# Half of a group's first layer by seven half-size products instead of eight, from the third group of tokens on

## The chip, the cores and the metric

The kernel is one program on one core of a Trainium2 chip. The metric is the device time of one execution in microseconds (us); for a kernel the median of several executions is given. A core has five engines that run their own instruction streams in order and wait for each other through semaphores: PE (TensorE, matrix products, with PEld its weight loads), DVE (VectorE), ACT (ScalarE), POOL (GpSimd) and SP (SyncE, which here issues all transfers). SBUF is the on-chip memory that they share; PSUM is a small memory of eight banks (128 x 512 floats each) into which PE writes and from which ACT and DVE read.

## What is computed

The program does attention inside chunks of 64 positions, and then a two-layer network on each of the 4608 tokens:

```python
scores = scale * np.matmul(q_c, k_c.transpose(0, 1, 2, 4, 3))   # chunks of 64, 8 batches x 8 heads x 9 chunks
attn = softmax(scores); out = np.matmul(attn, v_c)
x = out.transpose(0, 2, 1, 3).reshape(4608, 512)
h = x @ w_in                 # 512 x 2048, the first layer
g = h - np.tanh(h)
return g @ w_out             # 2048 x 512, the second layer
```

All inputs and the output are 32-bit floats. The kernel reaches their precision with two halves for each operand: a number is written as high part plus low part, and a product is three matmuls (high x high, low x high, high x low).

## The kernel before

**Tiling.** The tokens are cut into 36 tiles of 128 (a tile is called a pair, since it holds two chunks), and these into 9 groups of 4 tiles, so a group is 512 tokens. The 2048 hidden units are cut into 16 slices of 128, called `fc`. One unit of work is one `fc` for one group.

**First layer** (`gemm1`, line 413): twelve matmuls in 16-bit floats, each 128 x 128 weights by 512 tokens: four slices of the 512 inputs, each with three combinations of high and low parts. They sum in one PSUM bank `ph`, of which there are two.

**Between the layers** (`shrink`): ACT takes the tanh from `ph` into `t` (line 421), DVE forms `ph - t` (422), ACT rounds the result to the high part `gh` (425), DVE takes the rest `gl` (426). **Second layer** (`gemm2`, line 434): for each of the group's four tiles three matmuls, 128 x 128 by 512 columns, in a 32-bit form (`fp32r`), into one of the four PSUM banks `po0` to `po3`, which collect all 16 `fc`. `finish` copies them out and SP stores them (lines 457 to 461).

**Order.** `FeedForward.run` goes over the 16 units of a group. At each step it emits the first layer of unit *s* and its `shrink`, then, since `LAG = 2`, the second layer of unit *s* - 2. The list `queue` holds the units whose second layer is still to come. Between these, `interleaved` sets pieces of the *next* group's attention (class `Late`) at fixed half steps (`BASE`, `LATER`, `STEPS`): `sums` of absolute values by ACT (96) whose maximum over all partitions POOL takes (103, `power`), `split` into high and low 16-bit parts (307 to 317), `scores` by PE (325), `softmax` on DVE and ACT (331 to 339), a rounding and a transpose by DMA (345 to 348), `values` by PE (359), and the copy of the result into the next group's operand `xh`, `xl` (362, 363).

**The first group** is different: the weights arrive as raw 64-bit words that DVE and ACT convert (`merged`, `weights`), while the attention of groups 0 and 1 runs (class `Early`). The list `PLAN` gives the order of that part; up to its bar PE and SP follow it literally. The scale of each pair of weight slices and of each group's values comes from `power`, that is from one POOL instruction (line 103), whose result DVE waits for (105).

**Who sets the order elsewhere.** Outside such literal stretches a scheduler orders each engine's stream by priority and by what it takes to be ready; the order is fixed when the program is built.

Of the kernel before, what the change touches and what calls it, by code (L numbers as in the profile page):

```python
# [11 lines left out]
F32 = mybir.dt.float32  # L12
# [3 lines left out]
U32 = mybir.dt.uint32  # L16
AF = mybir.ActivationFunctionType
ALU = mybir.AluOpType
# [19 lines left out]
RAW = 3  # L38
EARLY_FC = 8
# [6 lines left out]
BASE = (3, 9, 15, 21)  # L46
LATER = (8, 13, 18, 23)
STEPS = (0, 3, 4, 5, 10)
# [6 lines left out]
def attn_ffn_kernel(ctx: ExitStack, tc: tile.TileContext, qE, kE, vE, qL, kL, vL, w_in, w_out, out):  # L55
# [13 lines left out]
    ps_h = ctx.enter_context(tc.tile_pool(name="ps_h", bufs=2, space=PSUM))  # L69
    ps_a = ctx.enter_context(tc.tile_pool(name="ps_a", bufs=2, space=PSUM))  # L70
# [18 lines left out]
    def new_x():  # L89
        return tuple(xpool.tile([P, KC, MOST], F16, name=f"x{a}") for a in "hl")  # L90

    def spread(pool, a, out):

        shape = [a.shape[0], *a.shape[1:]]
        junk = pool.tile(shape, BF16, name=f"junk{math.prod(shape[1:])}", bufs=1)
        nc.scalar.activation(junk, a, AF.Abs, scale=2.0 ** -12, accum_out=out)  # L96
# [66 lines left out]
    class Early:  # L163
# [96 lines left out]
        def result(self, p, x, i):  # L260
            xh, xl = x
            d = self.st.pop(p)
            ps, to = d["vps"], d["to"]
            ts = slice(i * P, (i + 1) * P)
            nc.scalar.activation(xh[:, :, ts], ps, AF.Copy, scale=to)
            nc.vector.scalar_tensor_tensor(out=xl[:, :, ts], in0=ps, scalar=to, in1=xh[:, :, ts], op0=ALU.mult, op1=ALU.subtract)

    class Late:
# [4 lines left out]
        def __init__(self, pool):  # L273
            self.pool, self.st = pool, defaultdict(dict)
            self.raw = {n: pool.tile([P, MOST // P, H * CH], F32, name=f"raw{n}", bufs=1) for n in "qkv"}
            self.v16 = [[pool.tile([P, 2, 4, P], F16, name=f"v16{a}{i}", bufs=1) for a in "hl"] for i in range(2)]
            self.q16 = [[pool.tile([P, H, P], F16, name=f"q16{a}{i}", bufs=1) for a in "hl"] for i in range(2)]
            for t in self.v16[0] + self.v16[1] + self.q16[0] + self.q16[1]:
                nc.gpsimd.memset(t, 0.0)

        def load(self, p, i):
            for n, src in (("q", qL), ("k", kL), ("v", vL)):
                nc.sync.dma_start(out=self.raw[n][:, i], in_=src[p - NE])

        def sums(self, g, n):

            d = self.st[f"g{g}"]
            if n == "q":
                d["sums"] = self.pool.tile([P, 3], F32, name="sums", bufs=2)
            some = self.raw[n][:, :SIZES[g]]  # L290
            spread(self.pool, some, d["sums"][:, "qkv".index(n):"qkv".index(n) + 1])
            if n != "v":
                return
            d["to"], d["from"] = (self.pool.tile([P, 3], F32, name=m, bufs=2) for m in ("to", "from"))
            power(self.pool, "x", d["sums"], d["to"], d["from"])
            d["exp"] = self.pool.tile([P, 1], F32, name="exp", bufs=2)
            nc.vector.scalar_tensor_tensor(out=d["exp"], in0=d["from"][:, 0:1], scalar=scale, in1=d["from"][:, 1:2], op0=ALU.mult, op1=ALU.mult)  # L297
            from_x[g] = d["from"][:, 2:3]

        def split(self, g, p, i):  # L300
            d, to = self.st[p], self.st[f"g{g}"]["to"]
            d["exp"] = self.st[f"g{g}"]["exp"]
            q, k = (self.raw[n][:, i].rearrange("p (h c) -> p h c", h=H) for n in "qk")
            qh, ql = self.q16[p % 2]
            for c in range(2):
                r = slice(c * CH, (c + 1) * CH)
                nc.scalar.activation(qh[r, :, r], q[r], AF.Copy, scale=to[r, 0:1])  # L307
                nc.vector.scalar_tensor_tensor(out=ql[r, :, r], in0=q[r], scalar=to[r, 0:1], in1=qh[r, :, r], op0=ALU.mult, op1=ALU.subtract)  # L308
            kk = d["k"] = self.pool.tile([P, 2, H, CH], F16, name="k16", bufs=2)
            nc.scalar.activation(kk[:, 0], k, AF.Copy, scale=to[:, 1:2])  # L310
            nc.vector.scalar_tensor_tensor(out=kk[:, 1], in0=k, scalar=to[:, 1:2], in1=kk[:, 0], op0=ALU.mult, op1=ALU.subtract)
            v = self.raw["v"][:, i].rearrange("p (a d) -> p a d", d=D)
            vh, vl = (t.rearrange("p c hp d -> p (c hp) d") for t in self.v16[p % 2])
            for u in range(2):
                r = slice(u * D, (u + 1) * D)
                nc.scalar.activation(vh[r, :, r], v[r], AF.Copy, scale=to[r, 2:3])  # L316
                nc.vector.scalar_tensor_tensor(out=vl[r, :, r], in0=v[r], scalar=to[r, 2:3], in1=vh[r, :, r], op0=ALU.mult, op1=ALU.subtract)  # L317

        def scores(self, p):
            d = self.st[p]  # L320
            ps = d["ps"] = ps_a.tile([P, H, CH], F32, name="psa")
            q = self.q16[p % 2]
# [18 lines left out]
        def transpose(self, p):  # L341
# [5 lines left out]
            aT = self.pool.tile([P, 8, P], F16, name="aT", bufs=1)  # L347
# [3 lines left out]
        def values(self, p, x, i):  # L351
            d = self.st.pop(p)
            xh, xl = x
            ps = ps_a.tile([P, 4, 2, CH], F32, name="psa")
            for hp in range(4):
                for c in range(2):
                    cs = slice(c * CH, (c + 1) * CH)
                    for k, (a, b) in enumerate(((0, 0), (0, 1), (1, 0))):
                        nc.tensor.matmul(ps[:, hp, c, :], lhsT=self.v16[p % 2][a][:, c, hp, :], rhs=d["a16"][:, b, hp, cs], start=(k == 0), stop=(k == 2))  # L359
            ts = slice(i * P, (i + 1) * P)  # L360
            ps = ps.rearrange("p hp c k -> p hp (c k)")
            nc.scalar.mul(xh[:, :, ts], ps, 2.0 ** -14)
# [233 lines left out]
```

## Time and profile before

| | |
|---|---|
| median of 3 runs | 894.82 us (892.93 to 894.85) |
| profiled execution | 890.42 us, its span (first to last instruction) 888.3 us |
| PE busy | 866.5 us of the span (98%), 5163 matmuls |
| DVE busy | 538.5 us (61%) |
| ACT busy | 471.3 us (53%) |
| POOL busy | 15.5 us (2%) |
| mean granted clock of PE | 0.989 of full speed |

The profiled execution is one run, with the chip's profiler on; it lies 4.4 us under the median. A row such as `504.26 1.04 PE L413 MATMUL ph<-xh,wih 128*128 128x512 f16 x4` of the timeline says: from 504.26 us on, 1.04 us long, four matmuls of line 413, which write `ph` from `xh` and `wih`. What stands in brackets at a row's end is how long the engine sat idle just before, and whose signal ended that. Matmuls overlap (the next is fed while the last drains), so their pace is read from start to start, not from a row's length.

### The profile page before, as it was taken

How to read it: one execution, taken by the hardware profiler on the slowest of the kernel's cores; microseconds unless marked ns; L12 is line 12 of the kernel's file. 1: busy time of each engine (PE TensorE's matmuls, PEld its weight loads, DVE VectorE, ACT ScalarE, POOL GpSimd, SP SyncE). 2: the span in 40 equal slices, each digit the busy share in tenths (PEclk: the TensorE clock that was granted, in tenths of full speed). 3: DMA queues.
4: the chain of work that ended last, by engine and by line, in shares of the span. 5: the costliest groups of instructions: out<-in, count | busy, mean ns of one | idle time of the engine just before them, and what ended most of it. 6: DMA issues, size and time to landing. Idle time of an engine off the chain costs nothing.

```text
span 888.3 us, 13109 instructions
## 1 busy us (share of the span) xinstructions
PE 866.5 (98%) x5163; PEld 566.8 (64%) x5163; DVE 538.5 (61%) x976; ACT 471.3 (53%) x824; POOL 15.5 (2%) x32
## 2 busy tenths in 40 slices
PE   7999898999999999999999999999999999999997
PEld 4786655566656666666666666666666666665665
DVE  6798896667666665656466745674567456533222
ACT  8589773756646544555455634663366344423221
POOL 0000003000000000000000000000000000000000
PEclk8899999999999999999999999999999999999999
DMA  9584333312221121212112211132111100010001
GB/s 261 184 233 133 136 122 121 117 36 66 78 83 51 34 72 61 61 47 72 60 53 53 74 60 37 49 89 66 37 48 24 60 13 13 13 54 6 1 1 48
DMA packets 61373, 62.71 MB, mean 71 GB/s; under 512 B 32640, under 2 KB 40832, under 8 KB 61312
## 3 DMA queue, kind: packets, MB, share of 16 engines
q1 hardware_dynamic: 61312, 61.88, 23.8%
q8 instruction: 40, 0.66, 0.3%
q14 instruction: 21, 0.17, 0.1%
HBM read 45.09 MB, written 9.44 MB: 61 GB/s over the span
## 4 chain that ended last, share of the span: by engine, by line
PE 91%; ACT 4%; issue 2%; DVE 2%; DMA 0%; POOL 0%; ACTq 0%; DVEq 0%; POOLq 0%
PE po L434 42%; PE ph L413 40%; PE psa L359 2%; PE psa L325 2%; PE psa L258 2%; PE psa L210 1%; ACT junk L96 1%; ACT s L228 1%; PE ph L501 1%; ACT wih L152 0%; ACT w_out L126 0%; ACT s L241 0%; DVE w_out L127 0%; PE psa L160 0%; ACT w_in L126 0%
## 5 line engine op out<-in xcount | busy, mean ns | idle before, releaser
L434 PE MATMUL po<-woh,gh 128*128 128x512 f32 x576 | 245.6, 426 | 3.3 <-ACT gh L425 3.3
L434 PE MATMUL po<-wol,gh 128*128 128x512 f32 x576 | 225.9, 392 | 0.0
L434 PE MATMUL po<-woh,gl 128*128 128x512 f32 x576 | 225.8, 394 | 0.0
L422 DVE SCALAR_TENSOR_TENSOR t<-ph,sig,t 128x512 f32<-128x512 f32 (+1 forms) x148 | 108.7, 734 | 146.7 <-ACT t L421 146.5
L413 PEld LDWEIGHTS <-wih 128*128 128x128 f16 x1184 | 106.4, 98 | 137.4 <-issue 25.7
L421 ACT ACTIVATE t<-ph,sig 128x512 f32<-128x512 f32 (+1 forms) x148 | 99.8, 674 | 168.0 <-PE ph L413 167.7
L426 DVE TENSOR_TENSOR gl<-t,gh 128x512 fp32r<-128x512 f32 (+1 forms) x148 | 99.8, 675 | 111.4 <-ACT gh L425 111.2
L413 PE MATMUL ph<-xh,wih 128*128 128x512 f16 (+1 forms) x592 | 150.8, 377 | 5.5 <-ACT wih L152 5.5
L425 ACT CAST gh<-t 128x512 fp32r<-128x512 f32 (+1 forms) x148 | 89.4, 604 | 126.0 <-PE po L434 101.5
L413 PE MATMUL ph<-xh,wil 128*128 128x512 f16 (+1 forms) x592 | 149.3, 375 | 0.2 <-DVE wil L153 0.2
L413 PE MATMUL ph<-xl,wih 128*128 128x512 f16 (+1 forms) x592 | 148.5, 373 | 0.0
L434 PEld LDWEIGHTS po<-woh,gh 128*128 128x128 f32 x576 | 108.5, 188 | 34.4 <-ACT gh L425 5.7
L434 PEld LDWEIGHTS po<-woh,gl 128*128 128x128 f32 x576 | 108.0, 188 | 24.5 <-DVE gl L426 0.5
L434 PEld LDWEIGHTS po<-wol,gh 128*128 128x128 f32 x576 | 108.5, 188 | 21.5
L413 PEld LDWEIGHTS <-wil 128*128 128x128 f16 x592 | 58.0, 98 | 67.3 <-issue 1.1
L317 DVE SCALAR_TENSOR_TENSOR v16l<-rawv,to,v16h 64x512 f16<-64x512 f32 x56 | 41.8, 746 | 5.6 <-ACT v16h L316 4.7
L316 ACT ACTIVATE v16h<-rawv,to 64x512 f16<-64x512 f32 x56 | 40.1, 716 | 6.0 <-PE psa L359 4.5
L307 ACT ACTIVATE q16h<-rawq,to 64x512 f16<-64x512 f32 x56 | 40.3, 720 | 4.3 <-DVE exp L297 3.2
L308 DVE SCALAR_TENSOR_TENSOR q16l<-rawq,to,q16h 64x512 f16<-64x512 f32 x56 | 41.6, 744 | 1.3
L345 ACT CAST a<-s 128x512 f16<-128x512 f32 x28 | 17.3, 616 | 30.7 <-DVE s L339 27.9
L333 ACT ACTIVATE s<-s,exp 128x512 f32<-128x512 f32 x28 | 20.1, 719 | 17.2 <-DVE s L332 17.1
L457 DVE COPY t<-po 128x512 f32<-128x512 f32 x18 | 12.4, 690 | 26.8 <-PE po L434 14.3
(98 smaller groups left out, 760.2 us busy)
## 6 DMA issues: line engine op xcount, KB each, us to landing
out<-t SPq DMA_DIRECT2D x36, 256.0 KB, 2.1
raw_in<-w_in SPq DMA_DIRECT2D x16, 512.0 KB, 5.3
raw_out<-w_out SPq DMA_DIRECT2D x16, 512.0 KB, 3.8
rawq<-qL SPq DMA_DIRECT2D x28, 256.0 KB, 2.6
rawk<-kL SPq DMA_DIRECT2D x28, 256.0 KB, 3.0
rawv<-vL SPq DMA_DIRECT2D x28, 256.0 KB, 2.6
qbd<-qE SPq DMA_DIRECT2D x16, 128.0 KB, 4.4
k<-kE SPq DMA_DIRECT2D x8, 256.0 KB, 4.5
```

The costliest lines, as they stand in the source:

```text
L258: nc.tensor.matmul(ps[:, hp, cs], lhsT=d["v"][:, hp, :, c], rhs=d["aT"][:, hp, cs], start=True, stop=True)
L307: nc.scalar.activation(qh[r, :, r], q[r], AF.Copy, scale=to[r, 0:1])
L308: nc.vector.scalar_tensor_tensor(out=ql[r, :, r], in0=q[r], scalar=to[r, 0:1], in1=qh[r, :, r], op0=ALU.mult, op1=ALU.subtract)
L316: nc.scalar.activation(vh[r, :, r], v[r], AF.Copy, scale=to[r, 2:3])
L317: nc.vector.scalar_tensor_tensor(out=vl[r, :, r], in0=v[r], scalar=to[r, 2:3], in1=vh[r, :, r], op0=ALU.mult, op1=ALU.subtract)
L333: nc.scalar.activation(s, s, AF.Exp, scale=d["exp"])
L413: nc.tensor.matmul(ph, lhsT=wi[fc // 2][a][:, fc % 2, kc * P:(kc + 1) * P], rhs=x[b][:, kc, cols], start=(k == 0), stop=(k == 3 * KC - 1))
L421: nc.scalar.activation(t, ph, AF.Tanh, scale=sig)
L422: nc.vector.scalar_tensor_tensor(out=t, in0=ph, scalar=sig, in1=t, op0=ALU.mult, op1=ALU.subtract)
L425: nc.scalar.copy(out=gh, in_=t)
L426: nc.vector.tensor_sub(gl, t, gh)
L434: nc.tensor.matmul(self.po[t], lhsT=gg[a][:, ts], rhs=wo[fc][b], start=(fc == 0 and i == 0), stop=(fc == FC - 1 and i == 2))
```

## The change

For groups 2 to 8 the first layer is computed in blocks of four `fc`. A block is a product of a 2 x 2 matrix of weight blocks (the two halves of the 512 inputs by the two halves of the four `fc`: 256 x 256 each) with a 2 x 2 matrix of token blocks (halves of the inputs by halves of the 512 tokens). The plain way is eight products of such blocks. The change uses a scheme of the Strassen kind with seven products and sums of blocks before and after:

- **Sums of weights** (`sums_of_weights`, once, in group 1): POOL adds and subtracts quarters of the weights, ACT and POOL split the sums into high and low parts `ws`. One sum overwrites a quarter of `wi` that is used no more.
- **Sums of tokens** (`sums_of_quarters`, per group): the attention's result is kept in `xf` (in the place of raw values) and DVE subtracts quarters of it; `operand` splits the seven operands (four quarters and sums of them).
- **Sums of products**: three PSUM banks, `bank_a`, `bank_b`, `bank_e`. A product adds into what a bank holds already; ACT copies `bank_a` into `bank_b`, copies `bank_b` out to `u` and `v` in SBUF, and DVE adds `bank_e` to these.
- **Order** (`Seven.run`): a product is twelve matmuls of 128 x 128 by 256 columns. After four of the seven products a `shrink` follows, on two `fc` by 256 tokens, as two tanh and two subtractions of 256 columns each and one rounding and one rest of 512. Each `shrink` puts two pieces of the second layer at the end of the list `pieces`; a piece is six matmuls of 512 columns for one tile. `piece()` takes the first of the list; eight of these calls stand in a block. The list goes on from group to group. PE follows the written order within a group (`manual_schedule`).
- **Room**: one buffer instead of two for the attention's PSUM bank, `q16`, `v16`, the exponents and `a`/`k`; three instead of two for `gh` and `gl`. The attention's steps stand at other places, its values are scaled and split later than its queries and keys, and `sums` is two calls.

```diff
-    ps_h = ctx.enter_context(tc.tile_pool(name="ps_h", bufs=2, space=PSUM))
-    ps_a = ctx.enter_context(tc.tile_pool(name="ps_a", bufs=2, space=PSUM))
+    ps_h = ctx.enter_context(tc.tile_pool(name="ps_h", bufs=1, space=PSUM))
+    ps_a = ctx.enter_context(tc.tile_pool(name="ps_a", bufs=1, space=PSUM))
+    bank_a, bank_b, bank_e = (ps_h.tile([P, MOST], F32, name=f"ph{n}") for n in "abe")
...
+        def operand(self, x, b, q):
+            h, l = (t[:, b].rearrange("p k (i t) -> p i k t", i=2) for t in x)
+            nc.scalar.copy(out=h, in_=self.quarter(q))
+            nc.vector.tensor_sub(l, self.quarter(q), h)
...
+        def sums_of_quarters(self, x):
+            b11, b21, b22, b12 = (self.quarter(b) for b in (B11, B21, B22, B12))
+            nc.vector.tensor_sub(b11, b12, b11)
+            self.operand(x, T1, B11)
+            self.operand(x, B22, B22)
+            nc.vector.tensor_sub(b12, b22, b12)
+            nc.vector.tensor_sub(b22, b22, b11)
+            self.operand(x, T2, B22)
+            self.operand(x, T3, B12)
+            nc.vector.tensor_sub(b21, b21, b22)
+            self.operand(x, T4, B21)
...
+    def sums_of_weights(pool, j):
+        h, l = wi[j]
+        f = [ffn.tile([P, 2, 2 * P], F32, name=n, bufs=1) for n in "uv"]
+        for i in range(2):
+            nc.gpsimd.tensor_add(f[i].rearrange("p a n -> p (a n)"), h[:, i], l[:, i])
+        (a11, a12), (a21, a22) = ((t[:, 0], t[:, 1]) for t in f)
+        nc.gpsimd.tensor_add(a22, a21, a22)
+        nc.gpsimd.tensor_sub(a21, a11, a21)
+        nc.gpsimd.tensor_sub(a11, a22, a11)
+        nc.gpsimd.tensor_sub(a12, a12, a11)
+        for at, src in ((slice(0, 2), f[0]), (2, a21), (None, a22)):
+            oh, ol = (wi[j][i][:, 1, 0:2 * P] if at is None else ws[j][i][:, at] for i in range(2))
+            nc.scalar.copy(out=oh, in_=src)
+            nc.gpsimd.tensor_sub(ol, src, oh)
...
+        def shrink(self, c, f_half, t_half):
...
+            for i in range(2):
+                sig = self.sig[:, 2 * self.block + i:2 * self.block + i + 1]
+                nc.scalar.activation(t[:, i], c[:, i], AF.Tanh, scale=sig)
+                nc.vector.scalar_tensor_tensor(out=t[:, i], in0=c[:, i], scalar=sig, in1=t[:, i], op0=ALU.mult, op1=ALU.subtract)
+            gh = ffn.tile([P, 2, MOST // 2], F32R, name="gh", bufs=3)
+            nc.scalar.copy(out=gh, in_=t)
+            gl = ffn.tile([P, 2, MOST // 2], F32R, name="gl", bufs=3)
+            nc.vector.tensor_sub(gl, t, gh)
+            fcs = [4 * self.block + 2 * i + f_half for i in range(2)]
+            for k in range(2):
+                Seven.pieces.append((self, fcs, 2 * t_half + k, k, (gh, gl)))
...
+            for self.block in range(FC // 4):
+                v, u = (ffn.tile([P, MOST], F32, name=n, bufs=1) for n in "vu")
+                self.product(bank_a, ("w", 0), B11, True)
+                nc.scalar.copy(out=bank_b, in_=bank_a)
+                piece()
+                self.product(bank_e, ("w", 2), T1, True)
+                piece()
+                self.product(bank_b, ("s", 0), T2, False)
+                nc.scalar.copy(out=v, in_=bank_b)
+                piece()
+                self.product(bank_a, ("w", 1), B21, False)
+                self.shrink(bank_a, 0, 0)
+                piece()
+                self.product(bank_b, ("s", 2), T3, False)
+                nc.scalar.copy(out=u, in_=bank_b)
+                nc.vector.tensor_add(u, u, bank_e)
+                self.shrink(u, 1, 1)
+                piece()
+                piece()
+                self.product(bank_b, ("w", 3), T4, False)
+                self.shrink(bank_b, 1, 0)
+                piece()
+                self.product(bank_e, ("s", 1), B22, False)
+                nc.vector.tensor_add(v, v, bank_e)
+                self.shrink(v, 0, 1)
+                piece()
```

**What moves on PE.** In the last group before, the first layer of a unit (bank `ph_8136`) is followed by the second layer of a unit whose tanh read `ph_8072`, two units earlier. The rows are PE's:

```order
L413 MATMUL ph_8136<-xl_6907,wih6_1102 128x512
L434 MATMUL po0_7771<-woh10_1097,gh_8088 128x512 [waits Activation_49]
L434 MATMUL po0_7771<-wol10_1099,gh_8088 128x512
L434 MATMUL po0_7771<-woh10_1097,gl_8089 128x512 [waits DVE_49]
...
L413 MATMUL ph_8168<-xh_6906,wih6_1102 128x512 [waits DVE_49]
```

In the changed kernel, same engine, last block of the last group: the product into `pha` (`bank_a`), then at once a piece that reads `gh_9756` and `gl_9758`; then the product into `phb` (`bank_b`), the second piece of the same pair, and a piece of `gh_9785`.

```order
L559 MATMUL pha_70<-xl_8077,wih7_1109 128x256
L588 MATMUL po0_9231<-woh12_1104,gh_9756 128x512 [waits Activation_49]
L588 MATMUL po0_9231<-wol12_1106,gh_9756 128x512
L588 MATMUL po0_9231<-woh12_1104,gl_9758 128x512 [waits DVE_49]
...
L559 MATMUL phb_71<-xl_8077,wsh7_1625 128x256
...
L588 MATMUL po1_9261<-woh14_1110,gl_9758 128x512
L588 MATMUL po2_9268<-woh13_1107,gh_9785 128x512 [waits Activation_49]
```

ACT's rows for the same place show where these operands come from: `t_9751` is the tanh of `pha`, `gh_9756` its rounding, `u_9682` the copy of `phb`, `gh_9785` the rounding of the tanh of `u`.

```order
L568 ACTIVATE t_9751<-pha_70,sig_9141 128x256 [waits PE_49]
L568 ACTIVATE t_9751<-pha_70,sig_9141 128x256 [waits DVE_49]
L571 CAST gh_9756<-t_9751 128x512 [waits DVE_49]
L627 COPY u_9682<-phb_71 128x512 [waits PE_49]
L568 ACTIVATE t_9780<-u_9682,sig_9141 128x256 [waits DVE_49]
L568 ACTIVATE t_9780<-u_9682,sig_9141 128x256
L571 CAST gh_9785<-t_9780 128x512 [waits DVE_49]
```

The piece that was two units behind its `shrink` now directly follows the product that this `shrink` reads; the second tanh from a bank waits for DVE's first subtraction from that bank.

**What moves on ACT in a block with attention** (first block of group 6): the split of the next pair's keys, `a_7221`, which waits for a DMA, stands between the tanh of `phb` and its rounding `gh_7206`.

```order
L368 CAST a_7180<-s_7162 128x512 [waits DVE_49,Activation_49]
L568 ACTIVATE t_7201<-phb_71,sig_6991 128x256 [waits DMAHW5_49,DMAHW2_49,PE_49]
L568 ACTIVATE t_7201<-phb_71,sig_6991 128x256 [waits DVE_49]
L330 ACTIVATE a_7221<-rawk_1628,to2_6913 128x512 [waits DMAHW7_49,Activation_49]
L571 CAST gh_7206<-t_7201 128x512 [waits DVE_49]
```

`a` holds both the rounded exponents, which the transposing DMA reads, and the next pair's keys, so the split waits for that DMA.

**What moves on POOL.** Before, at the start of the program, after the first instruction over all partitions (`ready`):

```order
L103 ISA wtop_264<-wsum_251 128x2 [waits Activation_49]
L103 ISA xtop_186<-vsum4_175 128x4 [waits Activation_49]
L103 ISA wtop_489<-wsum_476 128x2 [waits Activation_49]
L103 ISA wtop_659<-wsum_646 128x2 [waits Activation_49]
```

Now (line 103 has become 117), with the first sums of weights in between:

```order
L117 ISA wtop_266<-wsum_253 128x2 [waits Activation_49]
L527 ISA
L527 TENSOR_TENSOR u_1729<-wih0_73,wil0_75 128x512 [waits DVE_49]
L117 ISA
L117 ISA xtop_188<-vsum4_177 128x4 [waits Activation_49]
L527 ISA
L527 TENSOR_TENSOR v_1730<-wih0_73,wil0_75 128x512 [waits DVE_49]
L117 ISA
L117 ISA wtop_497<-wsum_484 128x2 [waits Activation_49]
```

The rows `ISA` without operands reload POOL's code: one library holds the reductions over partitions, another the additions. The program before has two such rows, both at its start; the changed one has them at each change between the two kinds, ten more among the early reductions and six after them, in group 1. The sums of the first weights are written in the program as a part of group 1; the scheduler has put them on POOL as soon as their inputs exist, between the reductions of the first group.

More of the change, by code (lines that the diff above doesn't have):

```diff
@@ L43 @@
 assert sum(SIZES) == NPAIR
[L46 to L48 removed]
+BASE = (0, 6, 12, 18)
+LATER = (6, 12, 18, 24)
+STEPS = (0, 3, 4, 5, 5, 8)
+SUMS = 28
+LATER_SUMS = 4
+B11, B21, B22, B12, T2, T3, T4 = range(7)
+T1 = B12
 PLAN = """
@@ L279, in __init__, with load @@
+            self.q16 = [pool.tile([P, H, P], F16, name=f"q16{a}", bufs=1) for a in "hl"]
+            self.xf = self.raw["v"].rearrange("p i (k t) -> p i k t", k=KC)
+            for t in self.v16 + self.q16:
                 nc.gpsimd.memset(t, 0.0)
-        def load(self, p, i):
+        def load(self, p, i, names="qkv"):
             for n, src in (("q", qL), ("k", kL), ("v", vL)):
[L283 to L298, printed above, removed]
@@ L406, in gemm1 @@
         def gemm1(self, fc, t0, t1):
-            cols, n = slice(t0 * P, t1 * P), (t1 - t0) * P
+            n = (t1 - t0) * P
             x = self.x
-            ph = ps_h.tile([P, MOST], F32, name="ph")[:, :n]
+            self.count += 1
+            ph = (bank_a, bank_b)[self.count % 2][:, :n]
+            halves = slice(t0 // 2, t1 // 2)
             k = 0
@@ L480, in attn_ffn_kernel @@
     att = Early(pool, [psum, ps_a], 4, warm)
-    idle = ps_h.tile([P, MOST], F32, name="ph")
+    idle = bank_a
     opened = ExitStack()
@@ L545, in attn_ffn_kernel @@
     raw_pool.close()
[L546 to L552 removed]
+    late = ctx.enter_context(tc.tile_pool(name="att", bufs=1, side="right", reuse_waits="tile"))
+    for j in range(FC // 2):
+        ws[j] = [late.tile([P, 3, 2 * P], F16, name=f"ws{a}{j}") for a in "hl"]
+    att = Late(late)
+    xs = [x, nx]
+    places = defaultdict(list)
+    for g in range(2, NG):
+        for k, fs in attention(att, g, xs).items():
+            places[k] += fs
+    for j in range(FC // 2):
+        places[1, 4 * j + 4].append(lambda j=j: sums_of_weights(late, j))
+    for g in range(1, NG):
+        if g + 1 < NG:
+            xs.append(new_x())
+        at = {k: places.pop((g, k)) for h, k in list(places) if h == g}
+        if g == 1:
+            ff = FeedForward(g, xs[g])
+            ff.room(ps_o1, range(2))
+            ff.room(ps_o2, range(2, 4))
+            ff.run([(fc, 0, 4) for fc in range(FC)], at)
+            continue
+        with tc.manual_schedule(engines={E.PE}):
+            Seven(g, xs[g], [ps_o1, ps_o1, ps_o2, ps_o2]).run(at)
+    assert not places
+    while Seven.pieces:
+        Seven.gemm2()
 def kernel(**inputs):
```

188 lines of the change are left out of this document (135 added, 53 removed).

## The prediction

> **What bounds the kernel now.** I read the page's busy line and chain first, then the stretches of one inner group and of the last group, and the pace of the matmuls in the timeline.
>
> ```profile
> PE 866.5 (98%) x5163; PEld 566.8 (64%) x5163; DVE 538.5 (61%) x976; ACT 471.3 (53%) x824; POOL 15.5 (2%) x32
> PE 91%; ACT 4%; issue 2%; DVE 2%; DMA 0%; POOL 0%; ACTq 0%; DVEq 0%; POOLq 0%
> core 0: us, PE busy (x) PEld busy (x) DVE busy (x) ACT busy (x) POOL busy (x), PEclk, DMA share, GB/s
> 337.00:429.00 92.00, 92.00 (x579) 59.41 (x578) 55.67 (x96) 48.15 (x72) 0.37 (x1) 1.00 0.20 59
> 337.93 7.79 PE ph L413 x36
> 429.69 7.79 PE ph L413 x36
> 504.26 1.04 PE L413 MATMUL ph<-xh,wih 128*128 128x512 f16 x4
> 505.13 1.03 PE L413 MATMUL ph<-xh,wil 128*128 128x512 f16 x4
> 509.63 1.04 PE L413 MATMUL ph<-xh,wih 128*128 128x512 f16 x4
> ```
>
> PE is the bound: busy in all of 92 us (fourth row: its window, then busy us and instructions of PE, PEld, DVE, ACT, POOL, the granted clock, DMA), and 91% of the chain that ended last. By the two rows of the chain of waits, successive groups begin 91.76 us apart (337.93, 429.69). A unit takes 509.63 - 504.26 = 5.37 us; four first-layer matmuls take 0.87, so twelve take 2.60 and the unit's twelve second-layer ones 2.77 (0.231 each). Sixteen units are 85.9 us; the other 5.8 of a group are its attention's matmuls. ACT and DVE are 52% and 61% busy there and never hold PE, because the second layer runs two units behind.
>
> **The matmuls removed.** Products of 256 columns exist already, in the first group:
>
> ```profile
> 37.74 0.60 PE L413 MATMUL ph<-xh,wil 128*128 128x256 f16 x4
> 38.18 0.60 PE L413 MATMUL ph<-xl,wih 128*128 128x256 f16 x4
> ```
>
> Four take 0.44 us, half of 0.87, so halving the width costs nothing. A product of twelve is 1.31 us, a piece of six second-layer matmuls 6 x 0.231 = 1.38. A block is 7 x 1.31 + 8 x 1.38 = 20.24 us of PE, against 4 x 5.37 = 21.48 for the four units it replaces: 1.24 saved, over 28 blocks (7 groups of 4) **-34.7 us**.
>
> **The waits added.** At each block start three pieces are left in the list: the calls take b1, v0, v1 (named after the bank or tile that their shrink reads; the end digit counts the pair), then a0, a1, u0, u1, b0. So a0 directly follows the product into `bank_a` whose shrink makes it; u0 is only one piece behind its product. PE runs in order: it stands until tanh, subtraction and rounding are done. The prices:
>
> ```profile
> 841.10 1.03 PE L413 MATMUL ph<-xl,wih 128*128 128x512 f16 x4
> 842.16 0.69 ACT L421 ACTIVATE t<-ph,sig 128x512 f32<-128x512 f32 x1 [2.21 <-PE ph L413]
> 842.89 0.75 DVE L422 SCALAR_TENSOR_TENSOR t<-ph,sig,t 128x512 f32<-128x512 f32 x1 [2.21 <-ACT t L421]
> L421 ACT ACTIVATE t<-ph,sig 128x256 f32<-128x256 f32 x8 | 3.8, 477 | 1.8 <-PE ph L413 1.6
> L422 DVE SCALAR_TENSOR_TENSOR t<-ph,sig,t 128x256 f32<-128x256 f32 x8 | 3.8, 480 | 0.9 <-ACT t L421 0.9
> L425 ACT CAST gh<-t 128x512 fp32r<-128x512 f32 x140 | 86.2, 616 | 126.0 <-PE po L434 101.5 <-DVE t L422 20.9 <-DVE sig L399 1.9
> L426 DVE TENSOR_TENSOR gl<-t,gh 128x512 fp32r<-128x512 f32 x140 | 96.5, 689 | 111.4 <-ACT gh L425 111.2
> L459 ACT COPY t<-po 128x512 f32<-128x512 f32 x18 | 10.5, 585 | 21.9 <-PE po L434 21.9
> L332 DVE TENSOR_TENSOR s<-psa,mx 128x512 f32<-128x512 f32 x28 | 19.0, 680 | 0.3
> 40.30 0.40 ACT L425 CAST gh<-t 128x256 fp32r<-128x256 f32 x1
> 40.75 0.50 PE L434 MATMUL po<-woh,gh 128*128 128x512 f32 x1 [0.58 <-ACT gh L425]
> ```
>
> The product's last column is fed at 841.10 + 0.87 = 841.97 and the tanh starts at 842.16: 0.19. ACT to DVE is 0.04 (842.85 to 842.89). From the end of `gh` (40.70) to the first matmul are 0.16: its row, 0.50 long, ends at 41.25, and a waiting-free one of these lasts 0.39.
>
> - a0: 0.19 + tanh 0.48 + subtraction 0.48 + tanh 0.48 + subtraction 0.48 (the second tanh waits for the first subtraction, as the order shows) + `gh` 0.62 + four handoffs of 0.045 + 0.16 = 3.07. The third matmul needs `gl` (0.69, begun when `gh` ends), 0.27 more. **3.3 us.**
> - u0: 0.19 + copy of `bank_b` 0.59 + addition of `bank_e` 0.68 + two tanh and subtractions, overlapped since `u` is in SBUF, about 1.4 + 0.62 + handoffs 0.13 + 0.16 = 3.77, less piece a1 (1.38), plus 0.27 for `gl`. **2.65 us.**
> - b0: the chain of a0, 3.07, less piece u1 and the last product (2.69), plus `gl`. **0.65 us.**
>
> Together 6.6 us: an uncovered block takes 26.85, 5.4 more than its four units. At group ends the next group's first product has slid into a0's wait and two pieces interleave, about 1.5 back each. 28 x 5.4 - 7 x 1.5 = **+140 us net**, the saving included. Below that it can hardly fall: only extra work for PE inside the waits would cover them, and the order has none.
>
> **Attention in the same queues** (six groups). ACT and DVE get per block three copies, two additions, and half-width instructions; per group seven operands where four results were. They stay under 75 us of some 120, so they aren't the bound, but whatever stands between a chain's links lengthens it.
>
> ```profile
> L310 ACT ACTIVATE k<-rawk,to 128x512 f16<-128x512 f32 x28 | 20.2, 722 | 0.7
> L317 DVE SCALAR_TENSOR_TENSOR v16l<-rawv,to,v16h 64x512 f16<-64x512 f32 x56 | 41.8, 746 | 5.6 <-ACT v16h L316 4.7
> aT<-a SPq DMA_TRANSPOSE x28, 3.1
> ```
>
> In a group's first block the exponents and one half of `v16` (0.72 each) precede the tanh of `u`, and two more such pairs `gh` and `gl`: about 2.1. The keys' split waits for the transpose (3.1 from issue to landing) ahead of `gh` of `bank_b`: about 1.7. Taken the same way, the second block gives about 1, the third 4 (the split between the two tanh of `bank_a`), the fourth 2.5 (two sums of 1.9 us on ACT). That is 11 if nothing ran early; none if everything did. I take 7: **+42 us** (0 to 66).
>
> **PE's clock.** Seen in stretches of 3.41 us:
>
> ```profile
> 97.16:100.57 3.41, 2.40 (x13) 2.01 (x13) 3.26 (x11) 1.55 (x5) 0.49 (x1) 1.00 0.81 299
> 138.12:141.53 3.41, 0.83 (x4) 0.37 (x2) 3.41 (x8) 1.38 (x3) 0.95 (x2) 1.00 0.98 355
> 141.53:144.94 3.41, 3.39 (x9) 1.19 (x10) 3.27 (x6) 1.10 (x2) 2.90 (x4) 0.50 0.23 84
> ```
>
> After a stretch with 0.83 us of work the next was granted half the clock; after one with 2.40 it kept the whole. A wait of 3.3 or 2.65 us leaves between 0.1 and 2.1 us of work in its worst stretch, between the two. A halved stretch costs up to 1.7. I take about one per block at 1.5: **+42 us** (0 to 80). The Trainium skill ("TensorE: Matmul & The Clock Gate", Part 1) says that the window is 3.4 us, free-running, and that the clock halves after an idle one; by it alone, waits shorter than a window would halve nothing and this term would be nearly none, but here 2.6 us of idling did.
>
> **POOL.** Sums of the first weights come between early reductions, with reloads of POOL's code:
>
> ```profile
> 7.88 0.28 POOL masks.py:199 TENSOR_SCALAR_AFFINE_SELECT ident<-ident 128x128 f32<-128x128 f32 x1 [6.95 <-issue]
> 14.88 0.38 POOL L479 PARTITION_ALL_REDUCE ready<-ready  x1 [6.71 <-DVE w_in L128]
> 17.19 0.37 POOL L103 PARTITION_ALL_REDUCE wtop<-wsum  x1 [1.94 <-ACT junk L96]
> 22.34 0.38 POOL L103 PARTITION_ALL_REDUCE xtop<-vsum  x1 [4.78 <-ACT junk L96]
> 22.75 0.16 DVE L105 TENSOR_REDUCE earlyfrom<-xtop 128x1 f32<-128x4 f32 x1 [0.89 <-POOL xtop L103]
> ```
>
> The two reloads there took 6.95 and 6.71. `xtop` moves from 22.3 to 17.6 + 6.9 + an addition of about 1 + 6.9 = 32.4, and DVE's queue with it, 10 us; some 5 of these fall into idling of DVE before 34 us. Later pairs of reloads (15 us) about fit the 12 to 16 us between reductions. I take **+5** (0 to 12). In group 1 five reloads delay the scales of group 2, and DVE's queue behind them, against two units of lead: **+3** (0 to 15). The first block of group 2 has no pieces in the list, and its sums of tokens come with the last attention step: **+6** (2 to 12).
>
> ```profile
> 136.51 2.84 DVE L127 TENSOR_SCALAR w_out<-w_out 128x512 uint32<-128x512 uint32 x1
> 137.16 1.02 POOL L279 MEMSET v16l<- 128x1024 f16 x1
> 143.22 0.68 DVE L137 TENSOR_TENSOR wol<-w_out,woh 128x512 fp32r<-128x512 f32 x1
> 142.93 0.95 POOL L279 MEMSET q16h<- 128x1024 f16 x1
> ```
>
> L127 stood 2.84 us beside POOL's fills, L137 ran undisturbed. The Trainium skill ("SBUF — State Buffer") says that DVE and POOL lock a shared pair of ports, and that DVE's two-input instructions collide with POOL only when POOL reads, as additions do and fills don't; no run here shows such a pair. By it group 1 would lose up to some 10 us more on DVE, mostly inside PE's lead.
>
> **Sum** against the profiled execution: 890.4 + 140 + 42 + 42 + 14 = 1128 us. That execution lies 4.4 under the median of 894.8; I leave this in the rounding. A change of 0.3% is about what can be told from none.
>
> **Rivals.** (1) The waits stand, but ACT and DVE keep up and the clock holds: 890 + 140 + 14 + 10 = about 1055. For it: DVE and ACT have a third of their time free. Chance 0.2. (2) Every long wait costs a halved stretch (two per block, 1.7 each: 95) and attention stands in each chain (66): 890 + 140 + 95 + 66 + 25 = 1215. Chance 0.13. (3) On the other side: the products' saving decides, because the pieces in the list are old enough when called; then 890 - 35 + 14 = 870. Its point of decision is the age of a0: it would need at least 3.1 us of other PE work between its product and its call, and the order shows none. Chance 0.03. (4) Narrow matmuls are held by their weight loads (98 ns each for 109 ns of columns) and save nothing: 35 more than forecast, 1163; the rows above speak against it. Chance 0.04. The forecast keeps 0.6.
>
> **Range and chances.** 1040 to 1205 holds the forecast, (1) and (4). Faster 0.03, same 0.01, slower 0.96.
>
> **What would show it.** PE busy near 75% in groups 2 to 8; waits of `po` (now line 588) on ACT `gh` of about 3 and 2.4 us, twice in every block, some 56 in all and some 28 short ones; blocks of 27 us in the last group, which has no attention; granted clock below 0.95 there, with stretches at 0.5; `xtop` near 32 us. If PE is 95% busy with `po` waiting for nothing, I am wrong.

## The result, and the profile after

| | before | after |
|---|---|---|
| median | 894.84 us (892.93 to 895.51, 4 runs) | 1191.88 us (1190.27 to 1197.84, 4 runs) |
| profiled execution, its span | 890.42, 888.3 us | 1197.84, 1196.0 us |

The changed kernel takes 1.3325 times as long, with a 95% interval of 1.3273 to 1.3377. The forecast was 1128 us, with a range of 1040 to 1205. The profiled execution after lies 6 us above its median and the one before 4.4 below, so the spans below differ by 10 us more than the medians.

PE's work became smaller and its share of the span fell. The busy line, the clock by slices and the chain from the page after:

```profile
PE 964.6 (81%) x6171; PEld 692.7 (58%) x6171; DVE 643.6 (54%) x1222; ACT 581.7 (49%) x1101; POOL 83.4 (7%) x107
PEclk6699999899899888898898889988889899899888
issue 58%; PE 24%; DVE 7%; ACT 6%; POOL 3%; DMA 1%; SPq 0%; POOLq 0%; ACTq 0%; DVEq 0%
```

PE shows more busy time than before because a matmul at half the clock is busy for longer: in `e3_older` below, at a mean clock of 0.96, the same matmuls are busy for 861.9 us. The chain's 58% of "issue" is no finding: from group 2 on it loses its thread in pieces of 40 to 90 us, so the stretches and the waits are read instead.

The stretches of the kernel before, group 1 and groups 2 to 8 (columns: window, its length, then busy us and instructions of PE, PEld, DVE, ACT, POOL, the mean granted clock, the share of DMA, GB/s):

```profile
154.41:246.17 91.76, 91.76 (x577) 59.25 (x576) 62.16 (x110) 59.73 (x88) 0.73 (x2) 1.00 0.27 77
246.17:888.30 642.13, 636.40 (x3840) 408.99 (x3838) 350.84 (x591) 299.01 (x451) 1.84 (x5) 1.00 0.16 46
```

The same of the kernel after, then groups 3 to 6 and the third block of the last group, which has no attention beside it:

```profile
167.88:284.69 116.81, 98.95 (x577) 62.56 (x575) 63.87 (x97) 61.33 (x101) 64.43 (x69) 0.94 0.14 40
284.69:1196.00 911.31, 720.00 (x4849) 524.90 (x4848) 451.81 (x842) 405.37 (x706) 3.99 (x11) 0.89 0.12 35
400.10:923.91 523.81, 414.24 (x2881) 303.13 (x2881) 275.79 (x516) 249.18 (x428) 2.88 (x8) 0.90 0.14 40
1125.96:1156.66 30.70, 26.12 (x133) 18.49 (x132) 7.75 (x14) 7.84 (x16) 0.00 (x0) 0.83 0.00 1
```

The program is 307.7 us longer by its spans. Group 1 begins 13.5 us later (167.88 against 154.41) and takes 25.1 us more (116.81 against 91.76). The start moves from run to run: in four more profiled kernels whose part up to there is the same but for at most one fill (`e1_fill`, `e2_fill_a`, `e3_older`, `e8_lag_four`) group 1 begins 7.0 to 12.7 us later than before. Its length there is 114 to 118 us. Groups 2 to 8 take 269.2 us more (911.31 against 642.13), with PE busy for 79% and a mean clock of 0.89.

PE's waits, longest in total first (us, times, longest):

```profile
PE po L588 <- ACT gh L571: 154.3, 58, 6.2
PE pha L559 <- DVE t L569: 22.7, 6, 3.9
PE pha L468 <- ACT xh L280: 10.6, 2, 10.0
PE po L588 <- DVE gl L573: 6.6, 12, 1.0
```

The first row is the wait that the prediction described: 58 times, about twice per block. One block of the last group shows both kinds, first on PE:

```profile
1165.92 0.38 PE L559 MATMUL pha<-xl,wih 128*128 128x256 f16 x2
1169.06 0.79 PE L588 MATMUL po<-woh,gh 128*128 128x512 f32 x1 [2.76 <-ACT gh L571]
...
1175.93 0.39 PE L588 MATMUL po<-woh,gl 128*128 128x512 f32 x1
1178.08 0.50 PE L588 MATMUL po<-woh,gh 128*128 128x512 f32 x1 [1.76 <-ACT gh L571]
```

and, for a0, the chain on ACT, which PE waits out:

```profile
1166.34 0.47 ACT L568 ACTIVATE t<-pha,sig 128x256 f32<-128x256 f32 x1 [2.08 <-PE pha L559]
1167.36 0.47 ACT L568 ACTIVATE t<-pha,sig 128x256 f32<-128x256 f32 x1 [0.55 <-DVE t L569]
1168.38 0.62 ACT L571 CAST gh<-t 128x512 fp32r<-128x512 f32 x1 [0.55 <-DVE t L569]
```

The product's last pair of matmuls starts at 1165.92, so its columns end at 1166.14. The piece starts at 1169.06, 2.92 us later. These waits halve the clock. The 3.41 us stretches around the same block, cut where the clock changes:

```profile
1161.65:1165.06 3.41, 3.41 (x24) 2.54 (x23) 0.00 (x0) 0.59 (x1) 0.00 (x0) 1.00 0.00 0
1165.06:1168.48 3.42, 1.24 (x12) 0.87 (x9) 0.97 (x2) 1.04 (x3) 0.00 (x0) 0.99 0.00 0
1168.48:1171.89 3.41, 2.83 (x7) 1.89 (x8) 0.69 (x1) 0.52 (x1) 0.00 (x0) 0.50 0.02 5
1171.89:1175.30 3.41, 3.41 (x16) 2.54 (x16) 0.08 (x1) 0.59 (x1) 0.00 (x0) 0.51 0.00 0
1175.30:1178.72 3.42, 1.66 (x7) 0.81 (x5) 2.16 (x4) 1.53 (x3) 0.00 (x0) 0.99 0.00 0
1178.72:1182.13 3.41, 3.41 (x12) 2.24 (x12) 0.03 (x1) 0.00 (x0) 0.00 (x0) 0.51 0.00 0
1182.13:1185.54 3.41, 3.41 (x25) 2.54 (x22) 0.97 (x2) 1.55 (x3) 0.00 (x0) 1.00 0.00 0
```

Three of the nine stretches of a block run at half the clock. The first follows the one with a0's wait (1.24 us of work). The second follows a stretch that was itself at half speed and still held part of that wait (2.83 us busy, worth 1.4 at full speed). The third follows u0's wait (1.66 us). A stretch full of work, even at half speed, brings the clock back.

### The profile page after: what moved, and what is told of

Same layout as the page of the kernel before. It is cut to its first block, busy times and chain, and to the rows that moved or that the text cites. A ratio compares the mean times of both kernels' runs of the same rounds, so it can differ in the third digit from the quotient of the medians.

```text
span 1196.0 us, 15627 instructions
## 1 busy us (share of the span) xinstructions
PE 964.6 (81%) x6171; PEld 692.7 (58%) x6171; DVE 643.6 (54%) x1222; ACT 581.7 (49%) x1101; POOL 83.4 (7%) x107
## 4 chain that ended last, share of the span: by engine, by line
issue 58%; PE 24%; DVE 7%; ACT 6%; POOL 3%; DMA 1%; SPq 0%; POOLq 0%; ACTq 0%; DVEq 0%
PE po L588 7%; PE po L489 3%; PE phb L559 3%; PE phb L468 2%; PE pha L468 2%; PE pha L559 1%; DVE t L569 1%; PE phe L559 1%; DMA s<-a 1%; ACT t L568 1%; PE psa L224 1%; ACT gh L571 1%; ACT junk L110 1%; PE psa L272 1%; POOL v L527 0%
## 5 line engine op out<-in xcount | busy, mean ns | idle before, releaser
L588 PE MATMUL po<-woh,gh 128*128 128x512 f32 x448 | 213.1, 476 | 154.8 <-ACT gh L571 154.3
L588 PE MATMUL po<-woh,gl 128*128 128x512 f32 x448 | 201.3, 450 | 7.9 <-DVE gl L573 6.6
L573 DVE TENSOR_TENSOR gl<-t,gh 128x512 fp32r<-128x512 f32 x112 | 77.2, 689 | 47.4 <-ACT gh L571 47.2
L571 ACT CAST gh<-t 128x512 fp32r<-128x512 f32 x112 | 69.0, 616 | 49.1 <-DVE t L569 48.3
L559 PEld LDWEIGHTS <-wsh 128*128 128x128 f16 x672 | 64.8, 107 | 34.7 <-issue 24.6
L568 ACT ACTIVATE t<-phb,sig 128x256 f32<-128x256 f32 x56 | 26.6, 474 | 112.3 <-PE phb L559 100.2
L569 DVE SCALAR_TENSOR_TENSOR t<-phb,sig,t 128x256 f32<-128x256 f32 x56 | 27.0, 483 | 92.2 <-ACT t L568 92.2
L559 PE MATMUL pha<-xh,wih 128*128 128x256 f16 x224 | 45.7, 287 | 22.7 <-DVE t L569 22.7
L628 DVE TENSOR_TENSOR u<-u,phe 128x512 f32<-128x512 f32 x28 | 19.1, 683 | 74.9 <-ACT u L627 74.9
L489 PE MATMUL po<-woh,gh 128*128 128x512 f32 x128 | 55.0, 430 | 0.9 <-ACT gh L479 0.9
L559 PE MATMUL phb<-xh,wsh 128*128 128x256 f16 x224 | 51.5, 317 | 2.0 <-ACT phb L616 2.0
```

Source lines behind the costliest of these rows:

```text
L489: nc.tensor.matmul(self.po[t], lhsT=gg[a][:, ts], rhs=wo[fc][b], start=(fc == 0 and i == 0), stop=(fc == FC - 1 and i == 2))
L559: nc.tensor.matmul(out[:, i], lhsT=w[:, kc * P:(kc + 1) * P], rhs=self.x[hx][:, b, kc], start=(start and i == 0 and k == 0), stop=(k == 5) ...
L568: nc.scalar.activation(t[:, i], c[:, i], AF.Tanh, scale=sig)
L569: nc.vector.scalar_tensor_tensor(out=t[:, i], in0=c[:, i], scalar=sig, in1=t[:, i], op0=ALU.mult, op1=ALU.subtract)
L571: nc.scalar.copy(out=gh, in_=t)
L573: nc.vector.tensor_sub(gl, t, gh)
```

## The experiments

Two theories stood against each other at first. One is the prediction's: pieces that are called too young make PE wait, and the waits also halve the clock. The other: the chains on ACT and DVE, with attention in between and tiles with a single buffer, are too long whatever PE does. The last part of the difference, before group 2, had its own two theories.

**More work for PE, in the waits.** Zero-weight matmuls ahead of a0 and u0 (`e1_fill`), or ahead of a0 alone (`e2_fill_a`, with 0 for 8):

```diff
+            z = Seven.zeros[0]
+            fill = {(0, 0): 12, (1, 2): 8}.get((fcs[0] % 4, t), 0)
+            for n in range(fill):
+                nc.tensor.matmul(self.po[t], lhsT=z, rhs=wi[0][0][:, 0], start=self.done[t] == 0 and n == 0, stop=False, skip_group_check=True)
```

> Twelve matmuls of 128x512 with weights of zero are added for PE ahead of piece a0, and eight ahead of piece u0, in every block; they add zero to the piece's own bank, so nothing else changes. Twelve are 12 x 0.2165 = 2.60 us, eight 1.73: a little less than the two waits of the last group's blocks (2.9 and 1.9 from the end of the last matmul to the next). Clock theory: of the 30.7 us of such a block some 4.6 are stretches at half clock, which come from the waits; with PE kept busy the clock stays at 1.0, a block takes 20.2 + 2.9 + 1.9 + about 0.9 of waits for gl and b0 = 26, and the kernel, though PE does 120 us more, becomes faster: 1192 - 28 x 4.6 = about 1063 (1050 to 1085). Rival, the halved stretches are no consequence of these waits, or the time is in the chains of ACT and DVE alone: 1185 to 1200; if the added matmuls come on top of the waits: 1192 + 121 = 1313.

> Only the twelve zero-weight matmuls ahead of a0. Clock theory: of three halved stretches per block, the two behind a0's wait go, the one behind u0's wait stays: some 3 of 4.6 us per block are gained, 1192 - 28 x 3.1 = about 1105. If a wait of 1.9 us does not halve the clock by itself, the third goes too: about 1065. Rival without the clock: 1185 to 1200.

Measured: 1141.37 us (1138.33 to 1144.40) for both places, and 1160.73 for a0 alone, in one run. With both, PE has 28 x 20 = 560 matmuls more to do, and the kernel becomes 50 us faster. A block of the last group with both fillings, and two of their rows:

```profile
1053.23:1080.15 26.92, 26.33 (x153) 17.71 (x153) 7.75 (x14) 7.84 (x16) 0.00 (x0) 1.00 0.00 1
```

```profile
1062.71 2.75 PE L589 MATMUL po<-wih,zeros 128*128 128x512 f16 x12
1065.63 0.50 PE L593 MATMUL po<-woh,gh 128*128 128x512 f32 x1 [0.17 <-ACT gh L572]
```

At a clock of 1.00 the block takes 26.92 us, with the same waits, now filled. That is 3.78 us less than the 30.70 of the changed kernel, and this difference is the clock's price in such a block. Filling a0's wait alone gives the same 26.91 in the block before last:

```profile
1068.31:1095.22 26.91, 24.59 (x146) 17.01 (x145) 7.76 (x14) 7.85 (x16) 0.00 (x0) 1.00 0.00 1
```

There the wait of u0 is open, and it cost nothing in clock; its stretch held 1.88 us of work. In the next block the stretch fell otherwise, held 1.50, and the next was halved:

```profile
1083.46:1086.87 3.41, 1.88 (x11) 1.24 (x8) 1.57 (x3) 1.58 (x4) 0.00 (x0) 1.00 0.00 0
1086.87:1090.28 3.41, 2.83 (x16) 1.94 (x17) 0.69 (x1) 0.53 (x1) 0.00 (x0) 1.00 0.00 0
...
1110.76:1114.18 3.42, 1.50 (x7) 0.88 (x6) 1.57 (x3) 1.98 (x4) 0.00 (x0) 1.00 0.00 0
1114.18:1117.59 3.41, 3.23 (x9) 2.16 (x10) 0.69 (x1) 0.13 (x1) 0.00 (x0) 0.52 0.00 0
```

The gain as a whole was overestimated (1063 and 1105 expected): the expectation counted every block as one of the last group. With both fillings a group with attention became only 3 to 10 us shorter, not the 15 of four such blocks, and PE still waited 51.3 us for `gh`, 51 times (154.3 and 58 without filling). That attention's matmuls and delays shift the waits, so that some of the filling stands where no wait is and comes on top, is likely but not shown.

**Older pieces.** The first two calls that would take a piece do nothing (`e3_older`), or only the first one (`e8_lag_four`, with `held = 1`); the list then holds five or four pieces at a block's start instead of three:

```diff
+        held = 2
...
             if not Seven.pieces:
                 return
+            if Seven.held:
+                Seven.held -= 1
+                return
```

> The first two calls that would take a piece do nothing, so that five pieces instead of three are left in the list at each block's start: a0 is then called after two other pieces and a product (1.38 + 1.31 + 1.38 = 4.1 us) and u0 after three pieces and two products. Nothing else changes, and three buffers of gh and gl are still enough. Theory (the age of the pieces is the cause): a block takes its 20.24 us of PE, the clock stays at 1.0: 284.7 to the start of group 2, + 28 x 20.24 + 6 groups x 5.8 of attention + about 7 at the end = 893 span, 895 us (885 to 915). Rival: attention's steps in the queues of ACT and DVE, with single buffers, hold the chains back in any case: waits of some us per block remain in the groups with attention and the clock drops with them, 940 to 1000.

> Only the first call is skipped in the changed kernel, so that four pieces are left in the list at a block's start. By the sums of the prediction: a0 is called after one piece and one product (1.38 + 1.31 = 2.69 us) with a chain of 3.07, so a wait of about 0.4 and 0.3 for gl remains; u0 is covered. A block without attention takes 20.4 + 0.5 to 0.7 = 21.0 us (20.40 with five pieces, 26.92 with three at full clock, 30.70 with three), and the clock stays at 1.0 there; the kernel 955 to 975. Rival, the wait has a fixed price whatever the age, or the clock drops with any wait: 24 us and more per block.

Measured: 949.24 us (945.26 to 953.42), a ratio of 1.0617 to the kernel before (1.0572 to 1.0662); and 985.0 in one run. Blocks without attention, with five pieces and with four:

```profile
874.82:895.22 20.40, 20.40 (x134) 16.15 (x133) 7.75 (x15) 7.86 (x15) 0.00 (x0) 1.00 0.00 1
```

```profile
910.74:931.76 21.02, 20.97 (x134) 16.08 (x133) 7.76 (x15) 7.87 (x15) 0.00 (x0) 1.00 0.00 1
```

So the price of a block follows the age of the pieces, as reckoned from a0: 26.92 with three pieces (at full clock), 21.02 with four, 20.40 with five. The sums gave 26.85, 21.0 and 20.24. A delay of two calls at the start of group 2, with no other change, takes 243 us off. With that the seven products do save PE time: 20.40 against the 21.48 of four units.

What is left was not expected in full (895 for five pieces, 955 to 975 for four). It is the rival's part, the waits that come with attention: in the last group, which has none, PE has no waits before the end, and in groups 3 to 6 it stands for about 2 us in three of a group's four blocks. Groups 3 to 6 with five pieces, and all of PE's waits there:

```profile
375.56:762.74 387.18, 361.52 (x2881) 283.26 (x2881) 267.76 (x517) 244.42 (x429) 2.89 (x8) 0.98 0.20 55
```

```profile
PE po L592 <- ACT gh L572: 7.9, 8, 1.7
PE psa L381 <- DMA s<-a: 7.8, 4, 2.0
PE pha L560 <- DVE t L570: 6.7, 4, 1.7
PE psa L348 <- ACT rawv L383: 3.3, 4, 0.8
```

A group takes 387.18 / 4 = 96.8 us, where PE's own work is 4 x 20.40 + 5.8 = 87.4. Of the 9.4 us, 6.4 are idling of PE ((387.18 - 361.52) / 4): about 2 each for `gh` and for the transposing DMA, 1.7 for the bank that DVE's subtraction still reads and 0.8 for attention's bank. Which step of attention holds each of these back was argued from the queues, not tested one by one. The clock of 0.98 costs part of the rest. Per group the kernel before had no such waits and took 91.76, so attention eats the saving.

**The sums of weights.** In the changed kernel the reductions of POOL come late, and in group 1 ACT stands for POOL's sums. From its timelines (POOL, then PE), and from its waits in group 1:

```profile
41.72 0.38 POOL L117 PARTITION_ALL_REDUCE xtop<-vsum  x1 [10.14 <-issue]
...
151.88 0.35 POOL L117 PARTITION_ALL_REDUCE wtop<-wsum  x1 [13.61 <-ACT junk L110]
...
205.35 1.40 PE L468 MATMUL pha<-xh,wih 128*128 128x512 f16 x4 [4.72 <-DVE t L477]
```

```profile
ACT wsh L535 <- POOL v L530: 17.1, 6, 4.6
ACT wsh L535 <- POOL u L532: 9.5, 6, 3.3
```

`xtop` came at 22.34 before. The last `wtop` before, from POOL's timeline:

```profile
135.88 0.52 POOL L103 PARTITION_ALL_REDUCE wtop<-wsum  x1 [13.94 <-ACT junk L96]
```

It comes 16 us later now; by the bracket in its row POOL itself waited 13.61 us for ACT's sum before it, so it was not POOL's queue that held this last one. In `e4_pool_rounds` POOL does the rounding, so that ACT and POOL wait for each other no more. In `e5_vector_sums` all additions and subtractions of the sums go to DVE and ACT rounds as before, in the kernel with five pieces; besides, only six of the eight pairs of weight slices stay in group 1, and these at every fifth half step instead of every fourth. The two diffs, one after the other:

```diff
-            nc.scalar.copy(out=oh, in_=src)
+            nc.gpsimd.tensor_copy(oh, src)
             nc.gpsimd.tensor_sub(ol, src, oh)
```

```diff
-        nc.gpsimd.tensor_add(a22, a21, a22)
+        nc.vector.tensor_add(a22, a21, a22)
...
-        places[1, 4 * j + 4].append(lambda j=j: sums_of_weights(late, j))
+        places[(1, 5 * j + 4) if j < 6 else (2, 8 * j - 41)].append(lambda j=j: sums_of_weights(late, j))
```

> In the sums of weights POOL also does the rounding to the high part that ACT did, so neither waits for the other there. In the changed kernel group 1 takes 127 us (157.7 to 284.7) against 91.8 before. Theory A: this comes from ACT standing in its queue for POOL's sums (17.1 + 9.5 + 4.6 us, with the shrinks of group 1 behind): group 1 comes to 92 to 105 us and the kernel to 1160 to 1172. Theory B: it comes from the reductions of POOL, late by the reloads of its code, and the scales that hang on them: POOL has even more to do, nothing is gained or some is lost, 1188 to 1205.

> The kernel with five pieces in the list, and the sums of weights on DVE in POOL's place (ACT still rounds them), those of the first six pairs in group 1 at every fifth half step, the last two behind the first two blocks of group 2. So POOL's code is reloaded at the start only, as in the kernel before. Theory A: the 13 us by which the last scale of the first weights comes later and the 25 us by which group 1 is longer in the changed kernel come from POOL's reloads and its long queue of additions; on DVE the sums are some 4 us for a pair, 24 in group 1, where DVE is busy for 62 of 92 us. Group 2 starts at 250 to 258 instead of 280, the kernel takes 918 to 930 instead of 949. Theory B: whatever engine does them, the sums hold the shrinks of group 1 in the queues of ACT and DVE: group 2 starts after 268, 940 to 960.

Measured: 1187.86 us (1183.36 to 1192.36), which is not told from the changed kernel's 1191.88; and 928.36 us (926.70 to 932.83), 21 less than with the sums on POOL. Group 1 in the two, and, for the second, groups 2 to 8:

```profile
160.20:270.81 110.61, 94.81 (x578) 61.01 (x575) 70.92 (x97) 52.57 (x78) 79.46 (x90) 0.94 0.16 42
```

```profile
160.46:254.00 93.54, 92.16 (x578) 59.03 (x575) 74.25 (x146) 58.59 (x96) 1.11 (x3) 1.00 0.17 44
254.00:924.80 670.80, 625.48 (x4849) 490.48 (x4848) 447.27 (x856) 400.90 (x711) 4.08 (x11) 0.98 0.17 48
```

(The first expectation counts group 1 of the changed kernel from 157.7, which lies inside the first group's last units; by the mark used here it is 116.81 us.) With the rounding on POOL, group 1 is 4 to 7 us shorter than in the changed kernel's five profiles, but still 18.8 us longer than before, outside the 92 to 105 of theory A of `e4_pool_rounds`: POOL is busy for 79 of 110 us, the reductions with their reloads stand in its queue, and the longest single wait of PE there is for the values' split, whose scale comes from such a reduction:

```profile
PE psa L381 <- ACT v16h L339: 10.3, 1, 10.3
```

With the additions on DVE group 1 takes 93.54, 1.8 more than before. Theory A of `e5_vector_sums` holds as a forecast (group 2 at 250 to 258, kernel 918 to 930): the sums' work on POOL was the cause in group 1. Three things went with it that this run does not separate: POOL's long queue, its reloads, and DVE's instructions that became slower beside POOL's additions (7.6 us, see the last section). Nor does it tell how much came from the two pairs that moved into group 2. Before group 1 the answer is weaker. Group 1 begins at 158.8 to 161.7 in the three kernels with the sums on DVE (this one, `e6_early_steps`, `e7_steps_rank`), at 160.20 with the rounding on POOL too, and at 161.4 to 167.88 in the five profiles with POOL and ACT as in the changed kernel, against 154.41 before. So some us of the early delay may be POOL's, but the ranges touch, and the cause of the rest stays open.

**Attention's places.** In the kernel of `e5_vector_sums`, the steps of attention moved:

```diff
-STEPS = (0, 3, 4, 5, 5, 8)
+STEPS = (0, 2, 3, 4, 5, 8)
```

for `e6_early_steps`, and (0, 3, 3, 4, 5, 8) for `e7_steps_rank`.

> As e5_vector_sums, with attention's steps at places 0, 2, 3, 4, 5, 8 instead of 0, 3, 4, 5, 5, 8 after a pair's start: scores, softmax and transpose one place (about 2.6 us) earlier against the values that wait for the transpose. With five pieces in the list, groups 3 to 6 take 95 to 99 us where PE's work alone is 4 x 20.4 + 5.8 = 87.4; PE waited 20 us for transposes and 15 for gh. If the lateness of attention's chain against PE's order is the cause, a group comes to 89 to 93 and the kernel to 15 to 30 us below e5_vector_sums. If ACT's and DVE's load in single-buffered tiles is, nothing changes (within 5), or the scores now wait for the split (slower by 5 to 15).

> As e5_vector_sums, with the steps at 0, 3, 3, 4, 5, 8: PE's scores stay where they are, only softmax and transpose are written one place earlier, so that the scheduler ranks them ahead of one more shrink. If rank in the queues is what makes the transposes late, 10 to 20 us below e5_vector_sums; if not, within 5 of it, or slower by the shrinks that now come later.

Measured: 960.38 us (959.74 to 961.01), 32 slower, and 922.02 (920.17 to 923.87), 6 faster, from two runs each. Neither met its forecast. With the scores earlier PE reaches them before attention's one bank has been read out, which no theory had named. This is PE's largest wait in that kernel; in `e5_vector_sums` it was 4.1 us in all:

```profile
PE psa L348 <- ACT rawv L383: 40.5, 19, 4.7
```

With the rank alone changed, the waits for the transposes fell from 14.0 us to under 1.3, but those for `gh` grew from 14.0 us to 20.9: as it seems, what attention gains in ACT's queue the chains of `shrink` lose. The 6 us lie between "10 to 20" and "within 5", and two runs are few, so a part for rank is likely and no more. This version is the fastest with the seven products, 3.3% over the kernel before (ratio 1.0327, 1.0292 to 1.0361). No run beats the kernel before.

## Why the prediction was right, and where it was off

The direction, the mechanism and the range held; the number was 64 us low. By the profiled executions the sum was 1128 - 890.4 = 238 us, against 307.

- **The saving of the products** was right. Products of 256 columns cost half of those of 512, and 20.40 us per block stand against the forecast 20.24 once nothing waits.
- **The waits** were right in place and size. Forecast: 5.4 us over the four units, 26.85 per block; measured at full clock: 26.92. In that block of `e1_fill` the piece a0 comes 2.92 us after its product's last column (forecast 3.07, without the wait for `gl`) and u0 2.27 after piece a1 (forecast 2.39). Over 28 blocks like this it would be 152 us of the 269.
- **The clock** was the right mechanism, but mis-sized. The term that was too small is "I take about one per block at 1.5: +42 us". In the last group there are three halved stretches per block, worth 3.78 us. Over groups 2 to 8 a mean of 0.89 means some 200 of 911 us at half speed (2 x 0.11 x 911). At the last group's rate (3 x 3.41 = 10.2 us at half speed for 3.78) these cost about 74 us; the most they can cost is 100. I had not seen that a halved stretch with part of a wait in it holds the clock down for one more, and took u0's wait for mostly harmless. The Trainium skill ("TensorE: Matmul & The Clock Gate", Part 1) has, in its table of states, the clock at half after at least one idle window. The trace shows more than that: no stretch around that block was idle, and 1.24 us of work did not save the next.
- **Attention in the queues.** What is left of the 269 is 269.2 - 152.3 - 74 = 43 us, for attention, the start of group 2 (forecast 6) and what groups give back at their ends (forecast -10.5). Forecast for the three were 37.5. That fits, but it is a remainder that takes over every error of the clock's term, and a count by groups doesn't bear it out: in the changed kernel a group with attention takes 127.4 to 132.9 us, where four blocks of the last group and attention's own matmuls come to 4 x 30.70 + 5.8 = 128.6. In `e1_fill`, at a clock of 0.95, it is 121.9 to 125.7 against 4 x 26.92 + 5.8 = 113.5, so 8 to 12 us more. In the changed kernel the clock's price and attention's overlap, and what each has of the sum is not separated. In `e3_older` attention costs 9.4 us per group, its share of the clock included.
- **POOL** was priced too low in group 1: "+3 (0 to 15)", where 25.1 was measured (23 to 26 in the five profiles). The reloads were priced, but not POOL's own queue of additions, with 64 us of work in group 1, nor ACT's standing in its order for the sums (27 us in the two rows above), with the shrinks of group 1 behind. "Two units of lead" covered less than that. For the early part, "+5 (0 to 12)", it was 13.5 in this execution and 7.0 to 12.7 in four others. In the three kernels with the sums on DVE, which have no reload there, 4 to 7 us are left, so no run shows the forecast term by itself.
- **What was to be seen**: 58 waits on `gh`, where some 56 were named; PE at 79% for 75%; `xtop` at 41.7 for 32; the clock at 0.89, with stretches at 0.5. Blocks of the last group took 30.7 and not 27, which is the clock's term again.

The rivals: (1) without the clock's price fell with the stretches at 0.50. (3), the pieces old enough, fell with the 58 waits; but its point of decision, 3.1 us of other work between a0's product and its call, proved right, since four pieces give 2.69 and leave a small wait, and five give 4.1 and leave none. (4), narrow matmuls, fell with 20.40. Of (2), the dear end, the last group shows even more than two halved stretches per block; the kernel as a whole lies between the forecast and it.

## What to carry to other kernels

A scheme that saves a few per cent of the work is worth less than the distance between a producer and its consumer in an engine's order: here two calls more or less decided over 243 us, and the saving was 30 (28 x 1.08). So count, for each result, how much other work stands on the engine between the last instruction it needs and the first that needs it, and compare that with the chain in between, before looking at the arithmetic. And a wait on PE is to be priced with the clock behind it: when waits cannot be avoided, even useless matmuls in them can pay.

## What the runs showed of the hardware

- A 3.41 us stretch need not be idle for the next one to be halved. The rows above have 1.24, 1.50 and 1.66 us of work at full clock followed by half, and 1.88 followed by full; a stretch at half clock kept the next at half with 2.83 us busy, and freed it with 3.41.
- Busy time is a poor measure of what decides this, since a record lasts until its last column has drained. Over all traces, from 290 us on, stretches at full clock with up to 1.92 us busy were followed by half and some with as little as 1.55 by full. Columns fed separate them better: each matmul's columns counted from its start at the pace of the rows, 512 in 0.2175 us at full clock and in twice that at half. Of some 1950 stretches at full clock all with fewer than 2980 columns were followed by half and all with more than 3140 by full; of some 200 at half clock, all up to 3157 kept the next at half and all from 3189 on freed it. So the border lies at 3000 to 3200 columns, well under half of the 8030 that fit into a stretch, and it is about the same at either clock. This is read off these traces and was not tested by a run of its own.
- Added work made a kernel faster: 20 zero-weight matmuls per block, 4.33 us, took 50 us off the whole.
- DVE beside POOL's additions. In group 1 of the changed kernel (186 to 232 us) one instruction that splits queries took longer than in group 1 of the kernel before, here in that order:

```profile
L328 DVE SCALAR_TENSOR_TENSOR q16l<-rawq,to,q16h 64x512 f16<-64x512 f32 x4 | 4.3, 1078 | 4.9 <-ACT q16h L327 4.8
```

```profile
L308 DVE SCALAR_TENSOR_TENSOR q16l<-rawq,to,q16h 64x512 f16<-64x512 f32 x12 | 8.9, 743 | 0.2
```

That is 0.34 us each, on four instructions. Over the whole of group 1 it adds up: `q16l` takes 0.997 against 0.743 before (8 times), `v16l` 1.079 against 0.746 (8), the rest `gl` 0.790 against 0.690 (16), the rounded exponents' rest 0.905 against 0.688 (4) and the keys' rest 0.852 against 0.749 (4), together 7.6 us, of the size of the "up to some 10 us" that the prediction set beside its sum. In `e5_vector_sums`, where POOL adds nothing, all five are back at 0.69 to 0.75. DVE's subtraction that reads one input from PSUM (`t`) stays at 0.74 to 0.75 in all three kernels.
